# Transposing u on the vector engine, with SBUF-to-SBUF gathers, in a fused attention and mixer kernel

## The chip, the cores and the metric

One core of a Trainium2 chip runs the whole program. The metric is the device time of one launch in microseconds; less is better. The core has a matrix engine (PE, with a separate weight load, PEld), a vector engine (DVE), a scalar engine (ACT), a general one (POOL) and a queue engine (SP) that here only issues copies to HBM. [...] Sixteen DMA engines carry all copies[...].

## What is computed

Sliding-window attention for 8 batches, 8 heads, 576 positions and head size 64, followed by a mixer over its output.

```python
scores = (1 / np.sqrt(D)) * np.matmul(q, k.transpose(0, 1, 3, 2))
rel = pos[:, None] - pos[None, :]
scores = np.where((rel >= 0) & (rel < 64), scores, -1e9)      # window 64
attn = exp(scores - max) / sum
x = np.matmul(attn, v)                                        # to [B, S, 512]
...
h = x.transpose(0, 2, 1) @ U @ V                              # mixes positions, rank 32
u = x + h.transpose(0, 2, 1)
out = u + np.maximum(u @ w_ch1, 0.0) @ w_ch2                  # 512 -> 2048 -> 512
```

Inputs and output are float32; the kernel computes in bfloat16 with float32 sums.

## The kernel before

The 8 x 576 = 4608 tokens are cut in 9 chunks of 512 tokens (CH), each of four tiles of 128 tokens (TPC). A batch has 4.5 tiles, so batches and chunks do not line up: tile g belongs to chunk g // 4. The mixer's two large products run by chunk, the attention by batch, and the loop at L655 interleaves them: pass c (0 to 8) computes the products of chunk c and, between their pieces, the attention of batch c + 1.

`mlp(c)` (L505) gives 32 pieces. The first 16 are `ch1(i)`: four matmuls of 128x512 into one PSUM tile psA, one for each 128 rows of the first weights w1b, with the transposed chunk uTc as the moving operand; then a relu on ACT, or on DVE for i in `DVE_RELU`, writes a c1 tile. The next 16 are `ch2(t, quarter)`: four matmuls each into psU for tile t; after the fourth quarter DVE adds u (L544) and SP issues the copy to HBM (L547). psA and psU share a pool of three buffers ("mm", L648). The pieces stand in 32 slots. The tables `PLACE`, `PLACE_1`, `PLACE_2`, `KT_3` and `KT_4` (L556 to L584) say behind which slot each step of the attention is issued: KT transposes k and q of a batch on DVE, S the scores with their exp on ACT and the mask on DVE, VC copies v, PV the product with v and its division, U the product with the matrix U, V the product with the matrix V with the add that gives a tile of u in SBUF (`un`, L431). The order of the instructions is written out by hand: each engine runs its own in the order of the program and waits on semaphores.

The first matmul needs u transposed, with the 512 features on partitions. `UT(t)` (L441) does it: four PE transposes of 128x128 into a PSUM tile and one copy by ACT into uTc; for batch 1 every second tile takes another PSUM pool (ps_big) and a DVE copy. There are 32 tiles of this kind. Chunk 0 goes another way, in the prologue: XT and UP (L469 to L492) multiply straight into the transposed form xT0, and four copies move it into uTc.

w1 comes in three loads (L195) and w2 in two, all on POOL's queue, and so do all loads of q, k and v; these are issued as soon as the buffers they write come free, which is often a pass before they are needed. q and k of batches 0 to 2 are read as pairs of bf16: their transposes move 32-bit elements, and the score matmuls then take every second element (L260).

Of the kernel before, what the change touches and what calls it, by code (L numbers as in the profile page):

```python
# [8 lines left out]
ACT = mybir.ActivationFunctionType  # L9
ALU = mybir.AluOpType  # L10

BF16 = mybir.dt.bfloat16
FP32 = mybir.dt.float32
# [3 lines left out]
def kernel(  # L17
# [11 lines left out]
    nc = tc.nc  # L29
    B, H, S, D = q.shape  # L30
    DM = H * D
    R = moe_U.shape[1]
    F = moe_w_ch1.shape[1]
    P = nc.NUM_PARTITIONS
    W = 64
    NB = S // W
    NDC = DM // P
# [9 lines left out]
    CH = 512  # L47
    TPC = CH // P
    NTOK = B * S
    NCH = NTOK // CH  # L50
# [8 lines left out]
    const = ctx.enter_context(tc.tile_pool(name="const", bufs=1))  # L59
    uT_pool = ctx.enter_context(tc.tile_pool(name="uT", bufs=3))  # L60
    u_pool = ctx.enter_context(tc.tile_pool(name="un", bufs=14))
    c1_pool = ctx.enter_context(tc.tile_pool(name="c1", bufs=1))
    wk_pool = ctx.enter_context(tc.tile_pool(name="wk", bufs=2))
    out_pool = ctx.enter_context(tc.tile_pool(name="osb", bufs=4))
    ps_big = ctx.enter_context(tc.tile_pool(name="ps_big", bufs=2, space=bass.MemoryType.PSUM))
    first = ExitStack()
# [8 lines left out]
    NT = 5  # L75
    ident = const.tile([P, P], BF16, name="ident")
    mask = const.tile([P, 2 * NB, W], BF16, name="mask")
    w1b = const.tile([P, NDC, F], BF16, name="w1b")
    w2b = const.tile([P, NFC, DM], BF16, name="w2b")
    ub = [const.tile([P, NT, R], BF16, name=f"ub{i}") for i in range(2)]  # L80
    vrep = const.tile([P, W + S + W], BF16, name="vrep")
# [106 lines left out]
    )  # L188
    nc.vector.tensor_copy(out=bias[:, NB:12, :], in_=bias[:, 6:NB, :])

    w1v = moe_w_ch1.rearrange("(c p) n -> p c n", p=P)
    w2v = moe_w_ch2.rearrange("(i p) m -> p i m", p=P)

    def load_w1(lo, hi):
        nc.gpsimd.dma_start(out=w1b[:, :, lo:hi], in_=w1v[:, :, lo:hi])  # L195

    def load_w2(lo, hi):
        nc.gpsimd.dma_start(out=w2b[:, lo:hi, :], in_=w2v[:, lo:hi, :])
# [11 lines left out]
    u_tiles = {}  # L210
    uT_tiles = {}

    def uT_of(c):
        if c not in uT_tiles:
            uT_tiles[c] = uT_pool.tile([P, NDC, CH], BF16, name="uTc")
        return uT_tiles[c]


    def attention(b, alone=False):
# [221 lines left out]
        def UT(t):  # L441
            def f():
                g = g0 + t
                wide = b == 1 and t % 2 == 1
                if wide:
                    tpb = ps_big.tile([P, 2, 2 * CH], BF16, name="tpw", tag="big")
                    tp = tpb[:, 0, 0:CH].rearrange("p (c q) -> p c q", q=P)
                else:
                    tp = psum["tp"].tile([P, NDC, P], BF16, name="tpu", tag="tp")
                for dc in range(NDC):  # L450
                    nc.tensor.transpose(  # L451
                        tp[:, dc, :], u_tiles[g][:, dc * P : (dc + 1) * P], ident[:]
                    )
                col = (g % TPC) * P
                copy = dve_copy if wide else nc.scalar.copy
                copy(out=uT_of(g // TPC)[:, :, col : col + P], in_=tp[:])  # L456
            return f

        pcs["KT"] = [KT(x, n) for n in range(NJ if pair else NJJ) for x in "kq"]
# [9 lines left out]
        def XT(t):  # L469
            def f():  # L470
                for dc in range(NDC):
                    nc.tensor.matmul(
                        xT0[dc // 2][:, dc % 2, t * P : (t + 1) * P],
                        x[:, t, 2 * dc : 2 * dc + 2, :].rearrange("p h d -> p (h d)"),
                        ident[:],
                        start=(t == 0),
                        stop=False,
                    )
            return f

        def UP():
            for dc in (0, 2, 1, 3):
                nc.tensor.matmul(
                    xT0[dc // 2][:, dc % 2, :],
                    hh["sb"][:, dc * P : (dc + 1) * P],
                    vrep[:, W : W + CH],
                    start=False,
                    stop=True,
                )
            for dc in (0, 2, 1, 3):  # L490
                copy = dve_copy if dc // 2 else nc.scalar.copy
                copy(out=uT_of(0)[:, dc, :], in_=xT0[dc // 2][:, dc % 2, :])  # L492

        pcs["XT"] = [XT(t) for t in range(NFULL)]
        pcs["UP"] = UP
        pcs["PV"] = [PV(t) for t in range(NT)]
        pcs["U"] = [UM((t,)) for t in range(NT)] if alone else [UM(tuple(range(NT)))]
        pcs["V"] = [VM((0, 1)), VM((2, 3)), VM((4,))]
        pcs["UT"] = [UT(t) for t in range(NT if odd else NT - 1)]
        return pcs  # L500


    DVE_RELU = (1, 4, 7, 10, 13)

    def mlp(c):  # L505
        uTc = uT_of(c)
        c1 = [None] * NFC

        def ch1(i):
            def f():  # L510
                ps = psum["mm"].tile([P, CH], FP32, name="psA", tag="mm")
                for dc in (0, 2, 1, 3) if c == 0 else range(NDC):
                    nc.tensor.matmul(  # L513
                        ps[:],
                        w1b[:, dc, i * P : (i + 1) * P],
                        uTc[:, dc, :],
                        start=(dc == 0),
                        stop=(dc == NDC - 1),
                    )
                c1[i] = c1_pool.tile([P, CH], BF16, name=f"c1_{i}")  # L520
                if i in DVE_RELU:
                    nc.vector.tensor_relu(out=c1[i][:], in_=ps[:])  # L522
                else:
                    nc.scalar.activation(out=c1[i][:], in_=ps[:], func=ACT.Relu)  # L524
            return f

        acc = {}

        def ch2(t, quarter):
            def f():  # L530
                g = c * TPC + t
                if quarter == 0:
                    acc[t] = psum["mm"].tile([P, DM], FP32, name="psU", tag="mm")
                for i in range(4 * quarter, 4 * quarter + 4):
                    nc.tensor.matmul(  # L535
                        acc[t][:],
                        c1[i][:, t * P : (t + 1) * P],
                        w2b[:, i, :],
                        start=(i == 0),
                        stop=(i == NFC - 1),  # L540
                    )
                if quarter == 3:
                    osb = out_pool.tile([P, DM], FP32, name="osb")
                    nc.vector.tensor_tensor(  # L544
                        out=osb[:], in0=acc[t][:], in1=u_tiles[g][:], op=ALU.add
                    )
                    nc.sync.dma_start(out=outf[g * P : (g + 1) * P, :], in_=osb[:])  # L547
            return f

        order = [(t, r) for t in range(TPC) for r in range(4)]  # L550
        if c == 0:
            order = [(t, r) for r in range(4) for t in range(3)] + [(3, r) for r in range(4)]
        return [ch1(i) for i in range(NFC)] + [ch2(t, r) for t, r in order]


    PLACE = {  # L556
        "VC": [0],
        "S": [1, 1, 4, 4, 7, 7],
        "PV": [10, 10, 13, 13, 15],
        "KT": [8, 9, 11, 12, 14, 15, 16, 18],  # L560
        "U": [17],
        "V": [19, 20, 22],
        "UT": [21, 22, 23, 24, 25],
    }
    PLACE_1 = {
        "KT": [13, 14, 15, 16],
        "S": [16, 16, 18, 18, 20, 20],
        "VC": [21],
        "PV": [23, 23, 25, 25, 26],
        "U": [28],  # L570
        "V": [29, 30, 31],
        "UT": [30, 31, 31, 32, 32],
    }
    PLACE_2 = {
        "KT": [1, 2, 3, 4],
        "S": [5, 5, 8, 8, 11, 11],
        "VC": [9],
        "PV": [14, 14, 16, 16, 18],
        "U": [20],
        "V": [22, 23, 24],  # L580
        "UT": [24, 25, 26, 27, 28],
    }
    KT_3 = [19, 20, 21, 23, 25, 27, 29, 30]
    KT_4 = [11, 12, 14, 16, 18, 19, 22, 25]  # L584


    def turn_over(n, cols=CH, to=None):
# [67 lines left out]
    for c in range(NCH):  # L655
        slots = [[] for _ in range(NSLOT + 1)]

        def place(b, parts, where):
            if b not in att:
                att[b] = attention(b)  # L660
            for part in parts:
                for f, s in zip(att[b][part], where[part]):
                    slots[s].append(f)

        b = c + 1
        if b == 1:
            for f, n in zip(att[0]["V"], (6, 8, 10)):
                slots[n].append(f)
        if b < B:
            if b == 1:  # L670
                load_kq(2)
            if b + 1 < B:
                load_v(b + 1)
            if b + 2 < B and b > 2:
                load_kq(b + 2)
            if b == 2:
                slots[5].append(lambda: load_kq(4))
            if b == 1:
                slots[23].append(lambda: load_kq(3))
            where = {1: PLACE_1, 2: PLACE_2}.get(b, PLACE)  # L680
            if b <= 2:
                place(b, ("KT",), where)
            place(b, ("VC", "S", "PV"), where)
            if 3 <= b + 1 < B:
                place(b + 1, ("KT",), {2: {"KT": KT_3}, 3: {"KT": KT_4}}.get(b, PLACE))
            place(b, ("U", "V", "UT"), where)
        for fill, extra in zip(mlp(c) + [lambda: None], slots):
            fill()
            for f in extra:
                f()  # L690
# [30 lines left out]
```

## Time and profile before

| | us |
|---|---|
| median of three runs | 331.75 |
| lowest, highest | 330.27, 332.63 |
| the profiled execution | 330.28 |
| its span, first to last instruction | 328.6 |
| PE psU and psA on the chain that ended last | 36%, 32% of the span |
| DMA on that chain (vA and kr loads) | 12% |

The passes of the loop can be told apart by their first psA and last psU matmuls: pass 0 runs from 24 to 64 us, pass 1 from 63.7 to 98.7, pass 2 to 132.9, pass 3 to 166.8, pass 4 to 201.3, pass 5 to 235.3, pass 6 to 269.4; passes 7 and 8, which have no attention, take 27.7 us each. The busy row gives each engine's share of the span. The row of slices cuts the span in 40 parts of 8.2 us and gives busy tenths. A group's line names the source line, the engine, the operation, the tiles and their shape, then total and mean time, and after the second bar the idle time ahead of it and what ended that. In the chain of waits each piece of work is listed with the start and the length that it adds to the end time, so overlapping matmuls are not counted twice.

### The profile page before, as it was taken

To read this page: it belongs to the slowest core of one execution; us is meant where nothing else is said; L and a number is where in the kernel's file an instruction comes from. 1 tells how busy PE (TensorE), PEld (TensorE's weight loads), DVE (VectorE), ACT (ScalarE), POOL (GpSimd) and SP (SyncE) were. 2 spreads that over 40 slices of the span, in tenths; PEclk is the share of its full clock that TensorE was granted. 3 is DMA by queue.
4 is the path that set the end of the run, shared out by engine and by line. 5 is a ranking of instruction groups with operands and counts; after the bars stand their busy time and mean duration, and the time that the engine had idled before them with its cause. 6 is when DMAs were issued, how large, how long until landed. Compare 5 with 4: busy or idle time off the path is not lost.

```text
span 328.6 us, 6914 instructions
## 1 busy us (share of the span) xinstructions
PE 318.5 (97%) x2949; PEld 156.3 (48%) x2949; DVE 195.1 (59%) x339; ACT 118.3 (36%) x188; POOL 83.0 (25%) x112
## 2 busy tenths in 40 slices
PE   8989989899999999999999999999999999999995
PEld 8544444454454545454544454445445444444442
DVE  7654759588787885689457955696456512212211
ACT  1524350365027423552246233732182224203400
POOL 8571419554626226125501400000000000000000
PEclk9999999999999999999999999999999999999999
DMA  7999999999999997999991911001100010021011
GB/s 120 156 199 209 206 137 173 206 197 141 170 189 180 181 111 96 203 105 63 176 225 13 73 64 67 1 2 55 75 2 0 34 66 30 2 89 39 2 64 64
DMA packets 96573, 34.34 MB, mean 105 GB/s; under 512 B 86688, under 2 KB 89888, under 8 KB 96544
## 3 DMA queue, kind: packets, MB, share of 16 engines
q0 software_dynamic: 91360, 24.48, 83.8%
q1 hardware_dynamic: 5184, 9.44, 8.3%
q8 instruction: 23, 0.38, 0.5%
q14 instruction: 6, 0.05, 0.1%
HBM read 48.94 MB, written 9.44 MB: 178 GB/s over the span
## 4 chain that ended last, share of the span: by engine, by line
PE 79%; DMA 12%; DVE 5%; POOL 2%; issue 1%; ACT 0%; DVEq 0%
PE psU L535 36%; PE psA L513 32%; DMA vA<-in_v_dram 7%; DMA kr<-in_k_dram 5%; PE xr L375 3%; PE sc L341 3%; PE psv L420 2%; PE tpu L451 2%; PE pshh L401 1%; DVE un L431 1%; POOL vA L124 1%; DVE xs L385 1%; DVE kt L243 0%; DVE qt L243 0%; DVE osb L544 0%
## 5 line engine op out<-in xcount | busy, mean ns | idle before, releaser
L535 PE MATMUL psU<-w2b,c 128*128 128x512 bf16 x576 | 135.1, 379 | 0.0
L513 PE MATMUL psA<-uTc,w1b 128*128 128x512 bf16 x576 | 131.4, 379 | 0.9 <-DVE uTc L492 0.6
L524 ACT ACTIVATE c<-psA 128x512 bf16<-128x512 f32 x99 | 59.3, 599 | 100.2 <-PE psA L513 99.6
L513 PEld LDWEIGHTS <-w1b 128*128 128x128 bf16 x576 | 53.9, 98 | 63.9 <-issue 1.7
L535 PEld LDWEIGHTS <-c 128*128 128x128 bf16 x576 | 53.6, 98 | 60.2 <-issue 3.0
L544 DVE TENSOR_TENSOR osb<-psU,un 128x512 f32<-128x512 f32 x36 | 24.8, 690 | 64.0 <-PE psU L535 63.9
L522 DVE TENSOR_SCALAR c<-psA 128x512 bf16<-128x512 f32 x45 | 30.8, 685 | 34.8 <-PE psA L513 34.6
L124 POOL DMA_DIRECT2D vA<-in_v_dram x32 | 28.4, 892 | 62.2 <-PE xr L375 19.8
L349 ACT ACTIVATE pts<-sc 128x768 bf16<-128x768 f32 x42 | 31.8, 808 | 11.8 <-PE sc L341 10.0
L456 ACT COPY uTc<-tpu 128x512 bf16<-128x512 bf16 x30 | 17.6, 586 | 40.3 <-PE tpu L451 40.3
L356 DVE TENSOR_TENSOR pts<-pts,mask 128x768 bf16<-128x768 bf16 x42 | 23.1, 557 | 12.2 <-ACT pts L349 9.3
L431 DVE TENSOR_TENSOR un<-psv,xs 128x512 bf16<-128x512 f32 (+1 forms) x40 | 25.7, 682 | 7.0 <-PE psv L420 6.8
L385 DVE TENSOR_TENSOR xs<-xr,rcp 128x512 bf16<-128x512 f32 (+1 forms) x40 | 27.6, 691 | 1.4
L112 POOL DMA_DIRECT2D kr<-in_k_dram x20 | 16.6, 828 | 21.8 <-DVE kt L243 8.8
L375 PEld LDWEIGHTS <-pts 128*64 128x64 bf16 x576 | 12.4, 110 | 10.4 <-DVE xs L385 5.2
L112 POOL DMA_DIRECT2D qr<-in_q_dram x20 | 16.5, 826 | 3.0 <-DMA vA<-in_v_dram 1.1
L243 DVE STREAM_TRANSPOSE kt<-kr 128x576 bf16<-128x576 bf16 x20 | 16.0, 799 | 0.0
L243 DVE STREAM_TRANSPOSE qt<-qr 128x576 bf16<-128x576 bf16 x20 | 15.7, 787 | 0.0
L375 PE MATMUL xr<-vB,pts 128*64 128x65 bf16 x320 | 15.4, 196 | 0.3 <-DVE vB L137 0.2
L341 PEld LDWEIGHTS <-kt 64*64 64x64 bf16 (+1 forms) x720 | 10.1, 105 | 10.8 <-issue 10.4
L410 ACT CAST hh<-pshh 128x512 bf16<-128x512 f32 x8 | 4.7, 586 | 28.9 <-PE pshh L401 28.9
L341 PE MATMUL sc<-qt,kt 64*64 64x128 bf16 (+3 forms) x720 | 12.9, 215 | 1.8 <-issue 1.4
(64 smaller groups left out, 161.8 us busy)
## 6 DMA issues: line engine op xcount, KB each, us to landing
out_dram<-osb SPq DMA_DIRECT2D x36, 256.0 KB, 2.0
kr<-in_k_dram POOLq DMA_DIRECT2D x26, 288.0 KB, 10.4
qr<-in_q_dram POOLq DMA_DIRECT2D x26, 288.0 KB, 11.4
vA<-in_v_dram POOLq DMA_DIRECT2D x32, 128.0 KB, 7.2
w2b<-in_moe_w_ch_dram POOLq DMA_DIRECT2D x2, 1024.0 KB, 19.2
w1b<-in_moe_w_ch_dram POOLq DMA_DIRECT2D x2, 512.0 KB, 9.6
w1b<-in_moe_w_ch_dram POOLq DMA_DIRECT2D x1, 1024.0 KB, 10.6
vB<-in_v_dram POOLq DMA_DIRECT2D x8, 64.0 KB, 7.8
```

Of the source, the lines that this page charges most:

```text
L112: nc.gpsimd.dma_start(out=dst[32 * part : 32 * (part + 1), off : off + NJJ * RD].rearrange("p (n x) -> p n x", x=r * D), in_=src[b, m * NJ ...
L124: nc.gpsimd.dma_start(out=va[:, t, :, 0:D], in_=v[b, :, t * P : (t + 1) * P, :].rearrange("h p d -> p h d"),)
L243: nc.vector.transpose(out=dst[:, n * S : (n + 1) * S].rearrange("q (m p e) -> q m e p", p=32, e=r), in_=src[:, 32 + n * RD : 32 + (n + 1) ...
L341: nc.tensor.matmul(sc[half * W : (half + 1) * W, g, (a - lo) * W : (z - lo) * W], operand("k", g, jj, e, kb * W, (kb + 1) * W), operand("q ...
L349: nc.scalar.activation(out=dst, in_=sc[:, :, 0 : PB * W].rearrange("p g (n w) -> p g n w", w=W), func=ACT.Exp, scale=scale,)
L375: nc.tensor.matmul(xr[r0 : r0 + W, h // 4, (h % 4) * VW : (h % 4 + 1) * VW], pts[:, g, jj * NB + blk, :], rhs, start=True, stop=True,)
L385: nc.vector.tensor_tensor(out=x[lo:hi, t, :, :].rearrange("p (a h) d -> p a h d", a=2), in0=xv[:, :, :, 0:D], in1=rcp[lo:hi].to_broadcast( ...
L431: nc.vector.tensor_tensor(out=u_tiles[g][rs, :], in0=ps[rs, n, :], in1=xt[n][rs], op=ALU.add)
L513: nc.tensor.matmul(ps[:], w1b[:, dc, i * P : (i + 1) * P], uTc[:, dc, :], start=(dc == 0), stop=(dc == NDC - 1),)
L522: nc.vector.tensor_relu(out=c1[i][:], in_=ps[:])
L524: nc.scalar.activation(out=c1[i][:], in_=ps[:], func=ACT.Relu)
L535: nc.tensor.matmul(acc[t][:], c1[i][:, t * P : (t + 1) * P], w2b[:, i, :], start=(i == 0), stop=(i == NFC - 1),)
```

## The change

For chunks 2 to 8 the PE transposes and their copies go. In their place `TR(g)` transposes a tile of u on DVE, as 32-bit elements (pairs of bf16) in blocks of 32x32, into a staging tile, and `gather(c)` moves the 16 blocks of a chunk, one copy for each pair of 32 source and 32 destination partitions, into uTc: eight issued on SP and eight on ACT. Since a pair of features stays together, partition p of uTc now holds features 2p and 2p + 1 of each half of 256. uTc has the form [128, 2, 512, 2] and w1b the form [128, 2, 2, 2048], its even and odd rows apart; each matmul reads every second element of uTc. For chunks 2 and up the tokens in uTc lie in the order of the gather, and the matmul reads them in token order. Chunks 0 and 1 keep their transposes on PE, with columns picked in the new order. w1 is loaded in two copies where it was one. The first two psA tiles of chunk 0 come from ps_big. The tables move most of S, PV, U and V one slot earlier and the later KT some slots later.

```diff
+    stg_pool = ctx.enter_context(tc.tile_pool(name="stg", bufs=2))
...
-    w1b = const.tile([P, NDC, F], BF16, name="w1b")
+    w1b = const.tile([P, 2, 2, F], BF16, name="w1b")
...
-    w1v = moe_w_ch1.rearrange("(c p) n -> p c n", p=P)
+    w1v = moe_w_ch1.rearrange("(g p e) n -> g p e n", g=2, e=2)
...
     def load_w1(lo, hi):
-        nc.gpsimd.dma_start(out=w1b[:, :, lo:hi], in_=w1v[:, :, lo:hi])
+        for g in range(2):
+            nc.gpsimd.dma_start(out=w1b[:, g, :, lo:hi], in_=w1v[g, :, :, lo:hi])
...
+    def halves(ap):
+        return ap.rearrange("p (g q e) -> g e p q", g=2, e=2)
...
-            uT_tiles[c] = uT_pool.tile([P, NDC, CH], BF16, name="uTc")
+            uT_tiles[c] = uT_pool.tile([P, 2, CH, 2], BF16, name="uTc")
...
-                        tp[:, dc, :], u_tiles[g][:, dc * P : (dc + 1) * P], ident[:]
+                        tp[:, dc, :], halves(u_tiles[g][:])[dc // 2, dc % 2], ident[:]
...
-                copy(out=uT_of(0)[:, dc, :], in_=xT0[dc // 2][:, dc % 2, :])
+                copy(out=uT_of(0)[:, dc // 2, :, dc % 2], in_=xT0[dc // 2][:, dc % 2, :])
...
-        pcs["UT"] = [UT(t) for t in range(NT if odd else NT - 1)]
+        pcs["UT"] = [UT(t) for t in range(NT - 1)] if b == 1 else []
...
+    def TR(g):
+        def f():
+            c, t = divmod(g, TPC)
+            if c not in stages:
+                stages[c] = stg_pool.tile([P, 8, TPC, 32, 2], BF16, name="stg")
+            nc.vector.transpose(
+                out=stages[c][:, :, t, :, :].rearrange("p j q e -> p j (q e)").bitcast(U32),
+                in_=u_tiles[g].bitcast(U32).rearrange("p (j x) -> p j x", x=32),
+            )
+
+        return f
+
+    def gather(c):
+        def f():
+            run = TPC * 32
+            for n in range(16):
+                i, j = (n + n // 4) % 4, n % 4
+                queue = nc.sync if n % 2 else nc.scalar
+                queue.dma_start(
+                    out=uT_of(c)[32 * j : 32 * (j + 1), :, i * run : (i + 1) * run, :].rearrange(
+                        "p g n e -> p g (n e)"
+                    ),
+                    in_=stages[c][32 * i : 32 * (i + 1)].rearrange(
+                        "p (g j) t q e -> p g j (t q e)", g=2
+                    )[:, :, j, :],
+                )
+
+        return f
...
+        def uT_cols(dc):
+            cols = uTc[:, dc // 2, :, dc % 2]
+            if c < 2:
+                return cols
+            return cols.rearrange("p (i t q) -> p t i q", i=4, t=TPC)
...
-                ps = psum["mm"].tile([P, CH], FP32, name="psA", tag="mm")
+                if c == 0 and i < 2:
+                    ps = ps_big.tile([P, 2, CH], FP32, name="psA0", tag="big")[:, 0, :]
+                else:
+                    ps = psum["mm"].tile([P, CH], FP32, name="psA", tag="mm")[:]
...
-                        w1b[:, dc, i * P : (i + 1) * P],
-                        uTc[:, dc, :],
+                        w1b[:, dc // 2, dc % 2, i * P : (i + 1) * P],
+                        uT_cols(dc),
...
-        "S": [1, 1, 4, 4, 7, 7],
-        "PV": [10, 10, 13, 13, 15],
-        "KT": [8, 9, 11, 12, 14, 15, 16, 18],
-        "U": [17],
-        "V": [19, 20, 22],
-        "UT": [21, 22, 23, 24, 25],
+        "S": [0, 0, 3, 3, 6, 6],
+        "PV": [9, 9, 12, 12, 14],
+        "KT": [8, 10, 11, 13, 15, 16, 20, 22],
+        "U": [16],
+        "V": [18, 19, 21],
...
-        "S": [5, 5, 8, 8, 11, 11],
-        "VC": [9],
-        "PV": [14, 14, 16, 16, 18],
-        "U": [20],
-        "V": [22, 23, 24],
-        "UT": [24, 25, 26, 27, 28],
+        "S": [5, 5, 8, 8, 10, 10],
+        "VC": [8],
+        "PV": [13, 13, 15, 15, 17],
+        "U": [19],
+        "V": [21, 22, 24],
...
-    KT_4 = [11, 12, 14, 16, 18, 19, 22, 25]
+    KT_4 = [11, 12, 14, 16, 20, 22, 24, 26]
...
-            place(b, ("U", "V", "UT"), where)
+            place(b, ("U", "V") + (("UT",) if b == 1 else ()), where)
+        if 2 <= c + 1 < NCH:
+            g0 = (b * S) // P
+            first = (c + 1) * TPC
+            last = max(first + t - g0 for t in range(TPC)) // 2 if b < B else 0
+            ready = where["V"][last] if b < B else 6
+            for t in range(TPC):
+                slots[ready - 1 + t // 2 if t < TPC - 1 else ready + 1].append(TR(first + t))
+            slots[ready + 2].append(gather(c + 1))
```

In pass 1, which prepares chunk 2, `ready` is 22: tiles 0 and 1 are transposed behind slot 21, tile 2 behind 22, tile 3 behind 23, and the gather is issued behind slot 24. In pass 2 `ready` is 19, in passes 3 to 6 it is 18, and in pass 7 it is 6.

More of the change, by code (lines that the diff above doesn't have):

```diff
@@ L455, in f @@
                 copy = dve_copy if wide else nc.scalar.copy
-                copy(out=uT_of(g // TPC)[:, :, col : col + P], in_=tp[:])
+                copy(
+                    out=uT_of(g // TPC)[:, :, col : col + P, :].rearrange("p g q e -> p g e q"),
+                    in_=tp.rearrange("p (g e) q -> p g e q", g=2),
+                )
             return f
@@ L473, in f @@
                         xT0[dc // 2][:, dc % 2, t * P : (t + 1) * P],
-                        x[:, t, 2 * dc : 2 * dc + 2, :].rearrange("p h d -> p (h d)"),
+                        halves(x[:, t, :, :].rearrange("p h d -> p (h d)"))[dc // 2, dc % 2],
                         ident[:],
@@ L484, in UP @@
                     xT0[dc // 2][:, dc % 2, :],
-                    hh["sb"][:, dc * P : (dc + 1) * P],
+                    halves(hh["sb"][:])[dc // 2, dc % 2],
                     vrep[:, W : W + CH],
@@ L498, in attention @@
         pcs["V"] = [VM((0, 1)), VM((2, 3)), VM((4,))]
-        pcs["UT"] = [UT(t) for t in range(NT if odd else NT - 1)]
+        pcs["UT"] = [UT(t) for t in range(NT - 1)] if b == 1 else []
         return pcs
     DVE_RELU = (1, 4, 7, 10, 13)
+    stages = {}
+    def TR(g):
[21 more added lines that the diff above has]
+                    )[:, :, j, :],
+                )
+        return f
     def mlp(c):
@@ L507, in mlp @@
         c1 = [None] * NFC
+        def uT_cols(dc):
[3 more added lines that the diff above has]
+            return cols.rearrange("p (i t q) -> p t i q", i=4, t=TPC)
         def ch1(i):
             def f():
-                ps = psum["mm"].tile([P, CH], FP32, name="psA", tag="mm")
+                if c == 0 and i < 2:
+                    ps = ps_big.tile([P, 2, CH], FP32, name="psA0", tag="big")[:, 0, :]
+                else:
+                    ps = psum["mm"].tile([P, CH], FP32, name="psA", tag="mm")[:]
                 for dc in (0, 2, 1, 3) if c == 0 else range(NDC):
                     nc.tensor.matmul(
-                        ps[:],
-                        w1b[:, dc, i * P : (i + 1) * P],
-                        uTc[:, dc, :],
+                        ps if c < 2 else ps.rearrange("p (t i q) -> p t i q", i=4, t=TPC),
+                        w1b[:, dc // 2, dc % 2, i * P : (i + 1) * P],
+                        uT_cols(dc),
                         start=(dc == 0),
@@ L521, in f @@
                 if i in DVE_RELU:
-                    nc.vector.tensor_relu(out=c1[i][:], in_=ps[:])
+                    nc.vector.tensor_relu(out=c1[i][:], in_=ps)
                 else:
-                    nc.scalar.activation(out=c1[i][:], in_=ps[:], func=ACT.Relu)
+                    nc.scalar.activation(out=c1[i][:], in_=ps, func=ACT.Relu)
             return f
@@ L566 @@
         "KT": [13, 14, 15, 16],
-        "S": [16, 16, 18, 18, 20, 20],
+        "S": [16, 16, 18, 18, 21, 21],
         "VC": [21],
         "PV": [23, 23, 25, 25, 26],
-        "U": [28],
-        "V": [29, 30, 31],
-        "UT": [30, 31, 31, 32, 32],
+        "U": [27],
+        "V": [28, 29, 31],
+        "UT": [29, 30, 31, 31],
     }
```

## The prediction

> **What bounds the kernel now.** I read the page's busy shares first, then its slices in time, then the matrix engine's forms.
>
> ```profile
> PE 318.5 (97%) x2949; PEld 156.3 (48%) x2949; DVE 195.1 (59%) x339; ACT 118.3 (36%) x188; POOL 83.0 (25%) x112
> ...
> PE   8989989899999999999999999999999999999995
> ...
> DMA  7999999999999997999991911001100010021011
> ...
> L456 ACT COPY uTc<-tpu 128x512 bf16<-128x512 bf16 x30 | 17.6, 586 | 40.3 <-PE tpu L451 40.3
> ```
>
> PE is full in every slice after the prologue, so an instruction taken from PE is time gained, and a wait put before PE is time lost one for one. ACT waits for the transposes; it holds nobody up. The DMA row matters as much: the 16 engines are full until about 172 us and nearly empty afterwards (a slice is 8.2 us). A copy added before 172 us meets other traffic, one added later does not.
>
> The chain of waits, asked for the second pass of the chunk loop (63.7 to 98.7 us), shows what a transposed tile costs on PE:
>
> ```profile
> 88.96 0.43 PE psv L420 x2
> 89.39 0.86 PE psU L535 x4
> 90.26 0.43 PE psv L420 x2
> 90.69 0.86 PE psU L535 x4
> 91.55 0.21 PE psv L420
> 91.77 0.22 PE tpu L451 x4
> 91.99 0.86 PE psU L535 x4
> 92.86 0.22 PE tpu L451 x4
> ```
>
> Columns: start, length, work. Without a transpose one slot (four matmuls) is 0.86 us; a tile's four transposes add 0.22 us. The 219 ns that the groups give for one transpose is pipelined and no price.
>
> The same pass, asked about the output copies on SP, and then the stretch from 200 to 300 us:
>
> ```profile
> DMA to landing us min/median/max: 5.5/6.8/8.0
> ```
> ```profile
> L547 SPq DMA_DIRECT2D out_dram<-osb x13: 332/332/333, 202.1 to 297.8; - x13
> ...
> DMA to landing us min/median/max: 2.0/2.0/2.3
> ```
>
> An issue holds its queue 0.33 us; the copy lands 2.0 us later on idle engines, about 6.8 us later in the full stretch. The packet records say where that goes: the first packet leaves 0.84 us after the issue when the engines are idle and 2.8 to 4.1 us after it when they are full. Last, the waits:
>
> ```profile
> POOL vA L124 <- DMA w1b<-in_moe_w_ch_dram: 5.3, 2, 4.1
> POOL kr L103 <- DMA w2b<-in_moe_w_ch_dram: 4.6, 1, 4.6
> ```
>
> These loads need nothing from the weights. Counted in order of issue, each waits for the load eight before it: the copies take eight semaphores in turn. In the records the output copies also use eight.
>
> [...] at its start 50 warm-up matmuls are 107 ns apart and the rest 56 ns, so one warm-up cost 50 x 0.051 = 2.6 us. [...] The score matmuls of batches 0 to 2 already read q in that step and show 219 ns for 128 columns against 220 without it; their ends are modelled, so this is weak support. [...]
>
> **The change part by part**, against the profiled execution: 330.28 us, span 328.6.
>
> *Transposes off PE.* 32 tiles go through UT now, 4 (batch 1) stay: 28 x 0.22 = **-6.2 us**, all on the path. The 28 ACT copies of 586 ns that go are worth nothing.
>
> *First two psA in ps_big.* The page's group of L513 has 0.6 us idle behind the DVE copy of uTc; a bank of its own can save about that: **-0.5** (0 to -0.9).
>
> *DVE.* 28 TR of 256 32-bit elements. Nearest rows: 799 ns (16-bit) and 1248 ns (32-bit) for 576, so 0.36 to 0.56; I take 0.5, four a chunk. DVE is busy 23 to 27 us of a 34 us pass, which hides 2 us, except where the gather waits behind it.
>
> *The gather, second pass (chunk 2).* It is hidden only if all 16 copies land before PE reaches chunk 2, since the first psA reads every partition and column. The pass ends at 98.7; four tiles less gives 97.8. DVE's list: V 0 in slot 21 releases two adds (88.5 to 89.9), TR 0 and 1 (90.9), two adds of V 1 (92.2), TR 2 (92.7), osb of slot 23 (93.4), a kt/qt transpose (94.2), TR 3 (94.7). Only 3.1 us are left, and the DMA row is full. Even on idle engines eight issues per queue (2.6) and a landing (2.0 less one issue) need 4.3 us. In the full stretch a 32 KB copy lands, by estimate, after 3.9 + 1.0 = 4.9 us (bounds 2.0 and 6.8). If SP and ACT share eight semaphores as POOL's loads do, copies 8 to 15 wait for copies 0 to 7, and copy 7 waits for the output copy of slot 23: issued 93.5, landed about 99.9; copy 7 lands 104.8, copy 15 109.7. Stall 109.7 - 97.8 = **+12**. If each queue could issue all eight at once: 94.7 + 2.3 + 4.9 = 101.9, stall 4. Behind ACT's gather stand the relus of the next chunk, which wait for PE anyway; behind SP's the output copies, with four osb buffers.
>
> *Clock.* [...] **+2.6** (0 to 2.6).
>
> *Other gathers.* Pass 2: TR 3 ends near 125.5, the DMA view of that pass shows the engines free from 122.6 to 127, two rounds need 5.3 us, the pass ends 131.8: hidden by 1 us. Pass 3: 9 us of slack, two rounds beside loads 10. Passes 4 to 6: DMA idle, 10 us of slack. Together **+0.5** (0 to 3). Pass 7 has no attention and its gather is at slot 8, between relus: ACT issues four, waits till 2.0, issues four more, so it is away 3.3 us. A slot is 0.86 us and psA has three buffers, so PE waits for relu 9: **+2.0** (0 to 3).
>
> *Prologue and placing.* w1 takes six issues instead of three (775 ns each on POOL), and their semaphore turns shift; the DMA engines are full there and bytes and order stay: **0** (-0.5 to 1). S, PV, U, V one slot earlier, some KT later: the same instructions, PE never idle there: 0 (-0.5 to 0.5). SBUF reads in pairs: 0; at worst a tenth of 576 matmuls of 216 ns, 12 us.
>
> Sum: -6.2 - 0.5 + 12 + 2.6 + 0.5 + 2.0 = **+10.4**, 340.7 us from the profiled execution. That one lies 1.5 us under the median of the three runs, 331.75; I say **341 us**.
>
> **Rivals.**
> (1) *One round.* SP and ACT need no turns: stall 4, clock 0 to 2.6, ACT 1.3, so -6.7 + 4 + 1.3 + 1.3 = about 0: 331 (329 to 334). For it: nothing shows SP ever waiting for a turn, its copies are far apart. Against: eight semaphores in the records.
> (2) *The gather is hidden: faster.* SBUF-to-SBUF copies get through the full engines as fast as through idle ones, and TR is at its short end, so that the gather ends 4.3 us after 94.1: stall under 1. With pass 7 at 1: -6.7 + 0.6 + 1 = -5, 326 us. Not slower holds as long as the stall in pass 1 and its clock cost stay under 6.7 - 2.5 = 4.2 us. For it: -6.2 is sure. Against: 3.9 us to the first packet in this very stretch.
> (3) *The matrix engine reads pairs slower, or the gather is late in several passes* (issue much over 0.33 us, more traffic per copy): +15 to +40, 346 to 370.
>
> **Numbers.** Chances: two rounds 0.45 (337 to 345), one round 0.2, hidden 0.25, worse 0.1. A measurement of this kernel tells some 1% (3.3 us) from no change. Faster over 1%, under 328.4: nearly all of hidden, 0.23. Within 1%, to 335.1: one round and some of two rounds, 0.21. Slower: 0.56. From 326 to 347 about 2 in 10 are left out: the lower part of hidden and all of worse. The likeliest case's own range is 337 to 345.
>
> **What would show it.** In the profile after: PE's transposes down to 16; a wait of PE for DMA before psA near 98 us, of 12 us for two rounds, 4 for one, none if hidden; psA matmuls 107 rather than 56 ns per 128 columns for some us after it; ACT's or SP's issues in two groups of four; psA spacing still 0.216 us; a gap of PE near slot 12 of pass 7. The prediction is wrong if chunk 2 starts within 4 us of the end of chunk 1.

## The result, and the profile after

| | us |
|---|---|
| before, median of 4 runs | 331.10 (330.27 to 332.63) |
| after, median of 4 runs | 371.06 (368.16 to 377.52) |
| ratio | 1.117, interval 1.109 to 1.126 |
| the changed kernel again, beside the experiments | 370.56, ratio 1.120 (1.116 to 1.125) |
| span of the repeat's profiled execution | 368.7 |

The change costs 40 us. In one of the four runs after, the slowest and the one profiled first (377.52, span 375.8), PE's clock was at most 0.95 of full speed from end to end, so the ratio leaves it out and every reading below is of the repeat's profile, in which the clock is whole except where it is spoken of.

The page of the repeat: busy shares, then the slices in time (one is 9.2 us), with the clock granted to PE and the share of the DMA engines.

```profile
PE 322.9 (88%) x2808; PEld 150.1 (41%) x2837; DVE 202.5 (55%) x367; ACT 102.2 (28%) x160; POOL 85.1 (23%) x115
...
PE   8899978999703999589994999999999999599995
...
PEclk9999999999965999979996999999999999899999
DMA  7999999999999164997799683300220040111002
```

Where PE was full in every slice, four holes now stand in its row, counted from slice 0: slices 11 and 12 (the wait begins at 99.4 us), 16 (152), 21 (194) and 34 (314). The first three lie where a pass hands over to chunk 2, 3 or 4, and the fourth is in pass 7. In or just after each hole the clock row drops. At the handovers to chunks 5 to 8, where the DMA row is nearly empty, there is no hole.

The longest waits of PE after the start, in the same trace (total, times, longest one, in us), are all of psA, the matmuls of ch1:

```profile
PE psA L560 <- DMA uTc<-stg: 22.1, 2, 17.0
PE psA L560 <- DMA out_dram<-osb: 5.8, 1, 5.8
PE psA L560 <- ACT c L571: 4.3, 1, 4.3
PE psA L560 <- DVE uTc L461: 1.4, 1, 1.4
```

17.0 is chunk 2, 5.1 (the rest of the first line) chunk 4, 5.8 chunk 3, and 4.3 the middle of pass 7: 32.2 us in all. The last line is in pass 0 and is taken up further down. The label of chunk 3 names an output copy, but what a psA matmul needs is the gather. Its last copy landed at 158.1, just before PE went on at 158.2.

The chain of waits between pass 1 and chunk 2 (start, length, work) is the predicted one:

```profile
94.29 7.19 DMA out_dram<-osb
101.48 0.02 issue
101.50 8.87 DMA uTc<-stg
110.36 0.02 issue
110.38 5.67 DMA uTc<-stg
116.06 0.35 issue
116.40 1.86 PE psA L560 x4
```

Three landings stand one behind the other: the output copy of slot 23, then copy 7 of the gather (numbered from 0) which waited for it, then copy 15 which waited for copy 7. The semaphores in the records bear it out: output copy, copy 7 and copy 15 are the first, ninth and seventeenth of a row that takes eight semaphores in turn, and all three bear the same one. Copies 8 to 14, on the other seven, were issued between 103.25 and 107.3.

The gather's part of that stretch, and last the windows of the trace after the wait. The window columns are start:end and length, busy time (count) of PE, PEld, DVE, ACT and POOL, then granted clock, DMA share and GB/s. The DMA share adds up the packets under way on the 16 engines, so it can pass 1.

```profile
L532 SPq DMA_DIRECT2D uTc<-stg x8: 585/586/926, 95.3 to 110.4; - x8
L532 ACTq DMA_DIRECT2D uTc<-stg x8: 592/652/920, 95.3 to 107.3; - x8
L519 DVE STREAM_TRANSPOSE stg<-un x4: 394/414/435, 91.4 to 94.9; 128x256 uint32<-128x256 uint32 x4
...
DMA to landing us min/median/max: 5.7/8.0/9.6
```
```profile
116.40:121.20 4.80, 4.80 (x36) 1.87 (x37) 1.35 (x3) 2.00 (x3) 0.00 (x0) 0.51 1.18 165
122.00:128.00 6.00, 6.00 (x77) 2.75 (x76) 2.16 (x4) 4.97 (x8) 0.00 (x0) 1.00 0.04 6
158.20:162.00 3.80, 3.80 (x33) 1.47 (x34) 0.52 (x1) 1.85 (x3) 0.00 (x0) 0.50 1.54 243
199.00:203.00 4.00, 4.00 (x34) 1.59 (x35) 0.62 (x2) 2.00 (x3) 0.00 (x0) 0.50 1.40 278
```

An issue holds its queue 0.6 us and a landing takes 8.0. After each wait PE works, without a gap, at half its clock: 4.7 us at the start of chunk 2, 3.9 of chunk 3, 4.1 of chunk 4, and 3.4 in pass 7, 16.0 us in all by the clock's own records, of which half is lost.

The last chunk, which no wait touches, shows one cost more. From the chain of waits of the kernel before (there chunk 7), and of the repeat (chunk 8):

```profile
269.43 13.81 PE psA L513 x64
283.24 13.81 PE psU L535 x64
```
```profile
336.46 14.50 PE psA L560 x64
```

A psA matmul takes 227 ns where it took 216. psU, whose operands are not pairs, keeps 216. Over 576 matmuls that is 6.3 us, as much as the transposes gave.

So the time adds up, from span to span: 328.6 - 6.2 (transposes, at the price of the prediction) + 6.3 (pairs) + 32.2 (the four waits) + 8.0 (half of 16.0 us) = 368.9, against 368.7 measured. The rest of the prologue and pass 0, 0.4 us net, is not in it: chunk 1 starts 1.1 us later than before, 0.7 of it by pairs.

### The profile page after: what moved, and what is told of

Read it like the earlier page. It is cut to its first block, busy times and chain, and to the rows that moved or that the text cites. A ratio compares the mean times of both kernels' runs of the same rounds, so it can differ in the third digit from the quotient of the medians.

```text
span 375.8 us, 6811 instructions
## 1 busy us (share of the span) xinstructions
PE 329.9 (88%) x2808; PEld 152.3 (41%) x2837; DVE 202.3 (54%) x367; ACT 102.2 (27%) x160; POOL 84.8 (23%) x115
## 3 DMA queue, kind: packets, MB, share of 16 engines
q10 hardware_dynamic: 4480, 1.84, 2.3%
## 4 chain that ended last, share of the span: by engine, by line
PE 64%; DMA 22%; DVE 6%; issue 2%; POOL 2%; SPq 2%; ACTq 1%; ACT 0%; DVEq 0%
PE psA L560 33%; PE psU L582 23%; DMA uTc<-stg 8%; DMA vA<-in_v_dram 6%; DMA out_dram<-osb 4%; DMA kr<-in_k_dram 4%; PE sc L346 3%; PE xr L380 3%; SPq L532 2%; DVE un L436 2%; PE psv L425 2%; DVE osb L591 1%; PE pshh L406 1%; DVE xs L390 1%; DVE stg L519 1%
## 5 line engine op out<-in xcount | busy, mean ns | idle before, releaser
L560 PE MATMUL psA<-uTc,w1b 128*128 128x512 bf16 x571 | 145.4, 403 | 34.3 <-DMA uTc<-stg 23.4
L582 PEld LDWEIGHTS <-c 128*128 128x128 bf16 x576 | 56.0, 100 | 71.7 <-issue 3.7
L346 PEld LDWEIGHTS <-kt 64*64 64x64 bf16 (+1 forms) x720 | 10.9, 111 | 11.4 <-issue 11.4
L346 PE MATMUL sc<-qt,kt 64*64 64x128 bf16 (+5 forms) x720 | 13.9, 224 | 0.8 <-issue 0.5
L380 PE MATMUL xr<-vA,pts 128*64 128x65 bf16 x256 | 12.8, 196 | 0.3 <-DVE xs L390 0.3
L425 PE MATMUL psv<-hh,vrep 128*128 128x512 bf16 x40 | 13.0, 390 | 0.0
```

Source lines behind the costliest of these rows:

```text
L346: nc.tensor.matmul(sc[half * W : (half + 1) * W, g, (a - lo) * W : (z - lo) * W], operand("k", g, jj, e, kb * W, (kb + 1) * W), operand("q ...
L380: nc.tensor.matmul(xr[r0 : r0 + W, h // 4, (h % 4) * VW : (h % 4 + 1) * VW], pts[:, g, jj * NB + blk, :], rhs, start=True, stop=True,)
L560: nc.tensor.matmul(ps if c < 2 else ps.rearrange("p (t i q) -> p t i q", i=4, t=TPC), w1b[:, dc // 2, dc % 2, i * P : (i + 1) * P], uT_col ...
L582: nc.tensor.matmul(acc[t][:], c1[i][:, t * P : (t + 1) * P], w2b[:, i, :], start=(i == 0), stop=(i == NFC - 1),)
```

## The experiments

Theory A: the turns of the eight semaphores and the slow landings beside POOL's loads make the waits, and the reading of pairs is a cost of its own. Rivals: B, the number and form of the copies, whatever else runs; C, the layout of the operands alone. The expectations call A "turns" and C "pairs", and name one rival more, "bytes": the 512 KB of a gather are slow beside the loads, in however many copies. The edits are against the changed kernel; the last but one is against the kernel before, and the last against the last but one.

**The changed kernel again**, as the base for all the others.

> The changed kernel once more, to have a profile at full base clock. Theory (turns): the gather's 16 copies and the output copies take eight semaphores in turn, and each turn is one landing beside POOL's loads. It expects 366 to 372 us, PE waiting about 19 us ahead of chunk 2, about 5 ahead of chunks 3 and 4, about 4 in pass 7, and half rate after each of these. Rival (bytes): the 512 KB themselves are slow beside the loads, whatever the number of copies; same numbers here. Rival (pairs): the even and odd reads slow the matmuls; it expects psA spaced wider than psU, which is 0.216 us in the kernel before.

370.56 us; it is the repeat read above.

**Eight copies of 64 KB.** Each takes one pair of partition groups, but half of all features, so blocks of u land in other places than the matmul wants.

```diff
-            run = TPC * 32
-            for n in range(16):
-                i, j = (n + n // 4) % 4, n % 4
+            run = TPC * 64
+            for n in range(8):
+                i, j, h = (n + n // 4) % 4, n % 4, n // 4
...
-                    out=uT_of(c)[32 * j : 32 * (j + 1), :, i * run : (i + 1) * run, :].rearrange(
+                    out=uT_of(c)[32 * j : 32 * (j + 1), :, h * run : (h + 1) * run, :].rearrange(
...
```

> The same 512 KB of a gather in 8 copies with runs of 1 KB instead of 16 with runs of 512 B, so that blocks of u land in other places than the reference wants. Turns: no second round inside a gather, only the wait of two copies for output copies stays; the wait ahead of chunk 2 falls from 19 to 8 us, those ahead of chunks 3 and 4 and in pass 7 to under 2; 342 to 350 us. Bytes: no change, 366 to 372 us. Pairs: no change.

346.14 us, ratio 1.045 (1.040 to 1.049). Its waits:

```profile
PE psA L560 <- DMA out_dram<-osb: 11.8, 2, 11.5
PE psA L560 <- ACT c L571: 1.5, 1, 1.5
PE psA L560 <- DVE uTc L461: 1.4, 1, 1.4
```

One turn is left: the eighth copy still waits for the output copy of slot 23 (issued 94.3, landed 103.4), and chunk 2 for the eighth copy, which landed at 110.6. The wait of 11.5 us is longer than the 8 expected. The waits of chunks 3 and 4 are all but gone (0.3 us), and that in pass 7 fell from 4.3 to 1.5. Bytes and pairs are the same, so half the copies, of twice the size, were worth 24 us. Each of them landed no sooner (median 9.2 us in that stretch), so the gain is in the turns and issues.

**Four copies of 128 KB**, one whole group of 32 partitions each, so no copy of the gather waits for a turn. Here too blocks land in other places than the matmul wants.

```diff
-            for n in range(16):
-                i, j = (n + n // 4) % 4, n % 4
+            for n in range(4):
+                i = (n + 1) % 4
...
+                    out=uT_of(c)[32 * n : 32 * (n + 1)].rearrange("p g n e -> p (g n e)"),
+                    in_=stages[c][32 * i : 32 * (i + 1)].rearrange("p j t q e -> p (j t q e)"),
```

> The same 512 KB in 4 copies of 128 KB, blocks in other places than the reference wants. Turns: the four copies take four free semaphores and wait for no output copy; issued by 98 us, landed by 103: the wait ahead of chunk 2 is 2 to 5 us, the others under 1; 330 to 338 us. Bytes: no change, 366 to 372 us. Pairs: no change.

340.01 us, ratio 1.029 (1.025 to 1.033). Waits and landings:

```profile
PE psA L555 <- DMA uTc<-stg: 5.2, 1, 5.2
PE xr L380 <- DVE vB L137: 2.9, 1, 2.9
```
```profile
DMA to landing us min/median/max: 7.6/8.1/8.7
```

A copy four times as large lands in the same 8 us, so neither "bytes" nor the size of a copy sets the landing. Nor, as far as was seen, do packets: by the pages ACT's gather copies take 80 each in the repeat (4480 for 56 copies) and 48 here (672 for 14), and those of the last experiment 144 (5760 for 40), which landed at a median of 5.6 us in pass 3 where the repeat's took 5.2. What in the loads makes the delay is not shown. The wait for the gather that is left is the one landing that TR 3 leaves no room for. The time is 2 us above the upper end expected, which did not count the pairs, nor the second wait: it is for a copy of v in pass 0, before any gather.

**No late loads.** The landings without POOL's traffic; the later batches work on the data of earlier ones.

```diff
-            if b + 1 < B:
+            if b + 1 < 3:
...
-            if b + 2 < B and b > 2:
+            if b + 2 < 5 and b > 2:
```

> Leaves out the loads of v from batch 3 on and of q and k from batch 5 on; those batches work on the data of earlier ones. The 16 copies of each gather stay. Turns: a landing takes 2 us instead of 5 to 9, so two rounds cost 6 to 8 us: the wait ahead of chunk 2 is 2 to 6 us, those ahead of 3 and 4 under 1, pass 7 as before at about 4; 334 to 345 us. Bytes: the same fall. Pairs: no change, 366 to 372 us.

342.49 us, ratio 1.036 (1.033 to 1.039), with all sixteen copies.

```profile
PE psA L560 <- ACT c L571: 4.2, 1, 4.2
PE psA L560 <- DMA out_dram<-osb: 3.3, 1, 3.3
```
```profile
DMA to landing us min/median/max: 1.9/1.9/2.2
```

The landings of that stretch (90 to 118 us) are those of idle engines. No gather copy has to wait for its turn any more, since the copy eight before it has landed when the queue is free. The 3.3 us left are eight issues on a queue (96.1 to 101.7) and one landing. So turns cost nothing at 1.9 us and much at 8; neither alone makes the 17 us. Against B: number and form of the copies are unchanged here. The wait in pass 7 stands, where no load ran before either.

**The layout alone.** Chunks 1 to 8 are transposed on PE again, with uTc and w1b in pairs; no TR, no gather.

```diff
-        pcs["UT"] = [UT(t) for t in range(NT - 1)] if b == 1 else []
+        pcs["UT"] = [
+            UT(t) for t in range(NT if odd else NT - 1) if (g0 + t) // TPC < 9
+        ]
...
-        if 2 <= c + 1 < NCH:
+        if 9 <= c + 1 < NCH:
...
```

> The change without its transposes on the vector engine: all 32 tiles go through PE as before; w1 in even and odd rows, uTc read in pairs, w1 in two copies, the first two psA in ps_big and the new places stay. Pairs (now with a number: psA matmuls stand 227 ns apart in the changed kernel and 216 in the one before): 576 x 0.011 = 6.3 us, and about 1 us in the prologue; 336 to 339 us, no wait of PE for DMA. If the pairs cost nothing by themselves: 329 to 332 us. Turns and bytes: nothing left of either.

338.15 us, ratio 1.024 (1.021 to 1.026): rival C is a part of the loss, not the loss. psA is 227 ns apart in every chunk, and PE has no gap over 1.3 us. Its span, 336.5, is 7.9 us above that of before; 6.3 of it is the spacing, and the other 1.6 is not assigned.

**The last gather later**, in pass 7 alone, where its tiles have long been there and the relus of psA no longer follow it.

```diff
-            ready = where["V"][last] if b < B else 6
+            ready = where["V"][last] if b < B else 14
```

> The changed kernel with the last gather (chunk 8) behind slot 16 of pass 7 instead of slot 8, so that no relu stands behind it on ACT. If ACT's issues and turns hold up the relus: the wait of 4.3 us and the half rate after it (1.7) go, 363 to 366 us. If PE waits there for something else: 368 to 372 us.

364.18 us, ratio 1.102 (1.099 to 1.106): 6.4 us less. The wait of pass 7 and the half rate behind it are gone (4.3 + 1.7 = 6.0), and from the start of chunk 7 to that of chunk 8 it is 28.3 us instead of 34.4. This is how it had looked in the repeat's timeline:

```profile
310.48 5.98 SPq L532 DMA_DIRECT2D uTc<-stg  x8
310.57 6.85 ACTq L532 DMA_DIRECT2D uTc<-stg  x8
...
317.52 1.57 ACT L571 ACTIVATE c<-psA 128x512 bf16<-128x512 f32 x3 [6.59 <-DMA uTc<-stg]
318.17 4.48 PE L560 MATMUL psA<-uTc,w1b 128*128 128x512 bf16 x12 [4.27 <-ACT c L571]
```

ACT issues copies for 6.85 us. Three relus pile up, all three psA buffers are full, and PE stands. Here the later issue is the faster one.

**Adjacent elements.** Step of two against the order of the runs: the matmul reads 512 neighbours (other elements than the product needs), everything else as it was.

```diff
-            cols = uTc[:, dc // 2, :, dc % 2]
+            flat = uTc[:, dc // 2].rearrange("p n e -> p (n e)")
+            cols = flat[:, (dc % 2) * CH : (dc % 2 + 1) * CH]
```

> The changed kernel with each matmul of psA reading 512 adjacent elements of uTc (in runs of 32, in the order of the gather) instead of every second one; these are other elements than the reference wants. If the step of two elements is what costs: psA spacing 216 ns, 6 us less, 363 to 366 us. If the order of the runs costs: spacing stays at 227 in chunks 2 to 8 and falls only in chunks 0 and 1. The waits for the gathers stay.

366.41 us, ratio 1.111 (1.106 to 1.116). The chain through the last chunk:

```profile
333.51 13.81 PE psA L561 x64
```

The spacing is 216 ns again in every chunk, so it is the step of two that costs. The span fell by 3.7 us (368.7 to 365.0) and not by 6.3. From the start of chunk 5 to the end the gain is whole, 2.8 us, the share of four chunks. Before that only 0.9 of 3.5 arrives: chunks 3 and 4 start when a gather lands, and each then runs longer at half rate (157.0 to 162.3 us instead of 158.2 to 162.0, and 197.3 to 203.3 instead of 198.9 to 203.0), 3.3 us more, of which half is lost. The rest is not assigned.

**Work in the wait.** 68, 18 and 16 matmuls that nothing reads, ahead of chunks 2, 3 and 4, keep PE running while it waits.

```diff
+        if c in (2, 3, 4):
+            unread = fresh()
+            turn_over({2: 68, 3: 18, 4: 16}[c])
```

> The changed kernel with 68, 18 and 16 matmuls of 512 columns on zeros put into the wait ahead of chunks 2, 3 and 4 (14.7, 3.9 and 3.5 us at 0.216; the waits are 17, 6 and 5.5), whose sums nothing reads. If half rate after an idle stretch is a cost of its own: no half-rate stretch ahead of chunks 2, 3 and 4, and 5 to 6 us less, 363 to 367 us. If the rate is not what costs there: 369 to 372 us.

367.23 us over four runs (363.6 to 371.7); the ratio, 1.109 (1.102 to 1.115), leaves out the highest. It lies just below the interval of the repeat, so the total leans to the first expectation and decides little. The profile decides in part: the mean clock rose from 0.951 to 0.986, and the half-rate stretches around the starts of chunks 2 to 4, which had lasted 17.1, 6.8 and 6.8 us, shrank to two of 3.4 us, where none was expected. And the waits did not close:

```profile
PE psA L560 <- DMA uTc<-stg: 7.2, 3, 3.1
```

The gathers landed later than in the repeat (median 8.7 us between 90 and 118, against 8.0). That idling brings the half rate is shown; that all 8 us can be had back by filling the wait is not.

**Late chunks only, no pairs.** From what was found: the kernel before, with TR and gather for chunks 5 to 8, where the DMA engines are idle; TR on single bf16 elements, so w1b and uTc keep their layout; the last gather at the later place; tables and psA0 as in the changed kernel.

```diff
+        pcs["UT"] = [
+            UT(t) for t in range(NT if odd else NT - 1) if (g0 + t) // TPC < 5
+        ]
...
+                stages[c] = stg_pool.tile([P, 16, TPC, 32], BF16, name="stg")
...
+                    out=uT_of(c)[32 * j : 32 * (j + 1), :, i * run : (i + 1) * run],
+                    in_=stages[c][32 * i : 32 * (i + 1)].rearrange(
+                        "p (g j) t q -> p g j (t q)", g=4
+                    )[:, :, j, :],
...
+        if 5 <= c + 1 < NCH:
...
+            ready = where["V"][last] if b < B else 14
...
```

> A version meant to keep the gain without its price: chunks 1 to 4 go through PE; chunks 5 to 8, when the DMA engines are idle, through DVE transposes of single bf16 elements and 16 copies each, into the plain layout of the kernel before (w1 in one copy, adjacent reads); the last gather behind slot 16 of pass 7. Turns: on idle engines two rounds with some 0.7 us per issue take 8 to 9 us of the 10 that are left in passes 4 to 6: no wait, 16 x 0.22 = 3.5 us less than before, 326 to 328 us. If the copies take longer with runs of 256 B: waits of 1 to 4 us in each of three passes, 330 to 340 us.

327.13 us, ratio 0.990 (0.988 to 0.992): 1% less than the kernel before. Its page:

```profile
PE 311.7 (96%) x2848; PEld 151.9 (47%) x2885; DVE 201.7 (62%) x355; ACT 108.9 (34%) x172; POOL 83.2 (26%) x112
...
PE   8889998999999999999999999999999999999995
...
PEclk9999999999999999999999999999999999999999
```

No hole, no drop of the clock. Sixteen tiles less on PE are 16 x 0.22 = 3.5. In passes 3 to 6, from which they went, the time fell from 136.6 to 133.3 us, by 3.3. The spans differ by 328.6 - 324.5 = 4.1 us; the rest lies ahead of pass 3, where the psA0 tiles and the moved tables were not tested apart. A 16-bit TR takes 681 ns instead of 414, which DVE has time for.

**The same from chunk 4**, one chunk earlier, where loads still run.

```diff
...
-        if 5 <= c + 1 < NCH:
+        if 4 <= c + 1 < NCH:
...
```

> The version with transposes of single elements and adjacent reads, now from chunk 4 on instead of chunk 5. Chunk 4's gather runs in pass 3 (near 157 us), beside POOL's loads. Turns: landings of 8 us there, two rounds 16 us of the 9 that are left: a wait of 5 to 8 us ahead of chunk 4 and half rate after it, 333 to 338 us. If the loads of that pass leave room: 325 to 327 us, 1 us less than from chunk 5 on.

336.55 us, ratio 1.020 (1.017 to 1.024). Waits and landings, the latter from 150 to 175 us:

```profile
PE psA L553 <- DMA uTc<-stg: 6.7, 1, 6.7
PE xr L376 <- DVE vB L137: 1.7, 1, 1.7
```
```profile
DMA to landing us min/median/max: 1.9/5.6/6.5
```

Four more tiles off PE (-0.9), a wait of 6.7, and 2.9 us of work at half rate behind it (173.1 to 176.0, +1.4) make 7.2 us. The span grew by 9.4, from 324.5 to 333.9. Chunk 1 had already started 1.7 later, after the second wait, for a copy of v in pass 0; the last 0.5 is not assigned. One gather in the wrong stretch undoes four in the right one.

## Why the prediction was wrong

It said 341 us, and 326 to 347. Slower was right, and so were the place and the mechanism of the longest wait; the size was not. From span to span 10.4 us more were forecast and 40.1 came. Of the 29.7 between, the other gathers make 10.4, the pairs 6.3, the clock 5.4, the gather in pass 1 5.0 and pass 7 2.3. By its steps:

- **Transposes off PE, -6.2**: right. The late-chunks kernel shows the price: 3.3 us for 16 tiles.
- **DVE**: right. TR took 414 ns, between the two ends; TR 3 was expected to end at 94.7, and the gather's first issues came at 95.3.
- **The gather in pass 1, +12**: right in its mechanism, two rounds of turns behind the output copy of slot 23. The mis-sized term is the landing: 4.9 us by estimate, from a first packet after 3.9 plus 1.0. The gather copies landed in 8.0 at the median, above even the upper bound of 6.8 taken from output copies. The output copy, copy 7 and copy 15 landed at 101.5, 110.4 and 116.1, where 99.9, 104.8 and 109.7 were forecast, and the stall was 17.0.
- **Other gathers, +0.5**: the step that failed. Pass 2 was to be "hidden by 1 us" and pass 3 to have about as much slack as its two rounds need. They waited 5.8 and 5.1 us. For pass 2 the prediction's own numbers say why. In the profile before, the DMA row from 115 to 133 us (a slice is 0.45 us) shows the engines free up to 127:

```profile
DMA  9999999999999726800000000006899999999999
```

The two rounds were to run from 125.5 to 130.8, so their second half lay beside loads, and was priced as if it did not. In the repeat the gather was issued from 145.8 to 151.2 and no copy waited for a turn, but POOL's loads began again at 148.6: the first ten copies landed in about 2 us, the last six in 4.2 to 7.7. An issue, too, was taken at the 0.33 us of an output copy and takes 0.6, so eight on a queue end 2.2 us later. In pass 3 the chain shows two rounds of 5.26 us. Rival 3 had named both causes ("issue much over 0.33 us", "late in several passes") and got a chance of 0.1; the 371 us lie just above even its 346 to 370.
- **Clock, +2.6 once**: right in kind. That a stall brings back what the 50 slow matmuls at the start cost was the author's estimate; in the repeat PE's first 3.4 to 4.7 us of work after a wait ran at half rate. But four waits came, and the total is 8.0 us. Nor did it take a long wait: in *Work in the wait* PE waited 3.1 us at most for a gather, and in the windows of the trace around the starts of chunks 2 and 3 (90 to 130 us and 130 to 170) the mean clock was 0.96, as one stretch of 3.4 us at half rate in each makes it.
- **Pass 7, +2.0**: right place and right cause, but 4.3 us and 1.7 of half rate. ACT was to be away 3.3 us and was away 6.85: seven of its eight issues took 0.6 to 0.8 us and one 1.7, the last for a reason that is not shown.
- **Prologue, 0, and psA0, -0.5**: chunk 1 began 1.1 us later than before (64.8 against 63.7), 0.7 of it by the pairs of chunk 0's 64 psA. The copies into uTc, which now write every second element, are longer: DVE's 722 ns instead of 422, ACT's 732 instead of 586. The wait of 1.4 us in the list above ends with such a DVE copy; in the layout alone, where it is 0.2, chunk 1 begins at 64.9 all the same. What the psA0 tiles save was not tested.
- **Pairs, 0**: wrong. 227 instead of 216 ns, +6.3 us, a twentieth of 576 x 216 ns, within the upper bound of a tenth. The 0 was the author's estimate. The trace's own evidence, 219 against 220 ns for 128 columns of score matmuls with modelled ends, was called weak and was taken all the same.

The waits of passes 1, 2, 3 and 7, and with them the clock, go back to two prices, landing and issue, that were both read from another kind of copy. The range fell short because the unknown prices enter four gathers together, while it treated them as separate mishaps.

## What to carry over

In this kernel the copies take eight semaphores in turn and a landing beside the loads (8.0 us) is slower than eight issues on a queue (5.6, in *No late loads*), so the sixteen copies ahead of chunk 2 cost a landing for each of their two rounds (8.9 and 5.7 us), and few large copies beat many small ones: 371 us with sixteen, 346 with eight, 340 with four. On idle engines, where one landed in 1.9 us, sixteen cost no wait from chunk 5 on. So read first how long a landing takes in the stretch, and where a free stretch ends. Price an issue and a landing from the same kind of copy at the same time of the kernel, and where one price enters several places, let all of them move together in the range. If an operand's layout has to change to make a cheap step possible, measure the layout alone: here it ate the whole gain.

## What the hardware showed

- Ahead of chunk 2, beside POOL's loads, the landing time of an SBUF-to-SBUF copy hardly depended on its size: 8.0 us for 32 KB (the repeat), 9.2 for 64 KB (*Eight copies*), 8.1 for 128 KB (*Four copies*), at the median. Without the loads a copy of 32 KB landed there in 1.9 us (*No late loads*).
- A 512-column matmul that read every second bf16 of its moving operand took 227 ns (the repeat and *The layout alone*) instead of 216 (the kernel before); with neighbours read from the same tile, 216 (*Adjacent elements*).
- An issue of a gather copy, from 32 partitions, held its queue 0.6 us (the repeat); an output copy from 128 partitions held it 0.33. The number of runs in a partition is not the reason: 0.6 with two runs each, 0.61 with four (the late-chunks kernel), and 0.57 to 0.95 with one (*Four copies*). What the reason is stays open.
- In this program SP's and ACT's copies, output copies and gathers alike, take the same eight semaphores in turn, so a late output copy held up a gather on another tile: in the repeat the output copy of slot 23 landed at 101.48 us, and copy 7 of the gather, on the same semaphore, was issued at 101.50.
- PE's granted clock stood at half for 17.1, 6.8 and 6.8 us around the starts of chunks 2 to 4 and for 3.4 in pass 7 of the repeat, in and after waits of 17.0, 5.8, 5.1 and 4.3 us. In *Work in the wait* waits of 3.1 us at most still brought two stretches of 3.4 us.
